# A new order table for the attention part, float64 conversion in three VectorE steps, and weight preparation moved

## The chip, the cores and the metric

The kernel runs on one core of a Trainium2 chip. Its engines work side by side, each through its own queue in program order: TensorE (PE) multiplies matrices, VectorE (DVE), ScalarE (ACT) and GpSimd (POOL) work element by element, SyncE (SP) issues most of the DMA transfers. The metric is the device time of one launch in microseconds (us); less is better.

## The reference

Attention with a learned position bias, for 4 batches, 8 heads, 576 positions and a head width of 64, then a block that mixes positions and applies an MLP. Cut to what is computed:

```python
scores = q @ k.T / sqrt(64) + bias        # bias[h,i,j] = relu(x[i,j]*w1 + b1) @ w2, hidden 32
attn = softmax(scores)                    # x = log1p(|i-j|) / log1p(max(i,1))
o = attn @ v                              # heads side by side: x is [4, 576, 512]
u = x + (x.T @ U @ V).T                   # mixes positions; U is 576x32, V is 32x576
out = u + relu(u @ w_ch1) @ w_ch2         # 512 -> 2048 -> 512
```

U, V, w_ch1 and w_ch2 come as float64. The kernel loads their two 32-bit words and puts a float32 together with bit operations.

## The kernel before, in words

**Stages.** First the bias table is built. Then come 16 pairs: a pair is one batch and two heads, p = 4 * batch + pair of heads. Then the MLP runs, its first steps (`m[0]`, `m[1]`, `y[0]`, ...) mixed with what is left of the last pair. The program is written with a manual schedule: each engine does its instructions in the order in which the code names them.

**A pair.** The 576 query rows of both heads make nine score tiles S0 to S8 (PE, L351); S0 holds the 64 middle rows of both heads. Each goes through T (DVE, L366: add the bias, find the maximum) and E (ACT, L384: exponential with row sums). The middle rows are normalised in PM (POOL, L405, two instructions, tile `pm`). X are transpositions on PE (L428, tile `tb`), C their copies out of PSUM (L411 on ACT, L413 on DVE); M and I are the same for the middle rows and the middle columns (tiles `tm`, `ti`), with CM and CI as their copies. AV0 and AV1 are the products with V (PE, L489), CO their copies (ACT), A0 and A1 transpose the outcome (tile `tx`), and D0 and D1 (DVE, L518, and for D0 also a small copy, L413) scale it into `x_sb`.

**Preparation of the next pair.** Q1 to Q4 split q and k of the next pair into a rounded part `hi` (L186) and a rest `lo` (L190) on POOL: hi of 1152 columns, lo of 1152, hi of 640, lo of 640. LA and LB are the loads of raw q and raw k for the pair after that, on SP's queue; the raw buffers are single, so such a load waits until the split of the pair before has read them.

**Float64 conversion.** From pair 2 on two jobs a pair are done, 20 in all (u, three pieces of v4, 16 pieces of the first MLP weights). VA: two steps on ACT (L206, L209). VD: clamp (DVE, L213) and shift (DVE, L218). VJ: join (DVE, L224) and the load of a later job. VP: add on POOL (L229) and what finishes the job before.

**Mix.** In pairs 5, 9 and 13, and after the last one, the four pairs of a batch are mixed: `mt` (PE, L538), `th` on ACT, `tl` on DVE, five products `mh` (PE, L560 to L562), five additions into `x_sb` (L566) and five stores to `u_dram`.

**What sets the order.** The table SLOTS names all of these for each slot 0 to 8 of a pair. One quote behind a name means the pair before, two quotes the one before that; `period(p, s)` walks through one slot. All outputs of PE take turns in one PSUM pool of four tiles, so that a new one waits until the one four places earlier has been emptied.

**Around it.** SP's list `loads` puts two more transfers into each slot (bias rows, raw q and k). In the last pairs `first_weights` brings in the converted first MLP weights, one step at a time (`next(feed, None)`): a load, a cast on ACT (L697, tiles `w1q`, `w2q`) and a subtraction on POOL (L698). `make_ut` (L687 to L690) transposes a block of u for the MLP.

Of the kernel before, what the change touches and what calls it, by code (L numbers as in the profile page):

```python
# [2 lines left out]

# [5 lines left out]
F32 = mybir.dt.float32  # L9
# [16 lines left out]
P = 128  # L26
# [15 lines left out]
CW = 256  # L42

SLOTS = (
    "S0 T8' D1'' E6' E7' E8'",
    "S1 T0 VD1' X20' E0 T1 MT MA C20' VP0' AV0' MD E1 N0 I1' CO0' H4 CI1' X30' VJ1' HD4 U4 H3 "
    "HD3 U3 N8' R8' C30' X31'",
    "S2 C31' Q1 H0 X21' C21' R0 PM",
    "S3 T2",
    "S4 HD0 U0 X00 T3 T4 VA0 H1 E2 E3 HD1 U1",  # L50
    "S5 AV1' E4 T5 C00 Q2 LA VD0 VJ0 A0' X11 Q3 CO1' I0 D0' C11 VP1' CI0 H2 HD2 U2 X01 X10 "
    "C01",
    "S6 M",
    "S7 C10 E5 Q4 LB",
    "S8 T6 T7 CM VA1 A1'",
)

CONV_FROM = 2
F64_LO = 2.0**-15
# [4 lines left out]
def kernel(  # L64
# [45 lines left out]

    ident = const.tile([P, P], F32, name="ident")
    sgn = const.tile([P, 1], I32, name="sgn")
    bits = const.tile([P, 8], I32, name="bits")
    three, mask, top = bits[:, 0:1], bits[:, 1:2], bits[:, 2:3].bitcast(F32)

    eps = const.tile([P, 9], F32, name="eps")[:, 0:1]
    u_sb = mix.tile([P, 5, RANK], F32, name="u_sb")
    v4h = mix.tile([P, 640], F32R, name="v4h")
    v4l = mix.tile([P, 640], F32R, name="v4l")
# [192 lines left out]
    def bias_loads(c, hp):  # L312

        h, r = 2 * hp, slice(c * P, min(S, (c + 1) * P))
        if c < 4:
            j = (1 + 2 * c) * S
            parts = [
                (bias[hp][:, j : j + S], bd[h][r]),
                (bias[hp][:, j + S + LEFT : j + 2 * S], bd[h + 1][r, 0 : S - LEFT]),
                (bias[hp][:, j + S : j + S + LEFT], bd[h + 1][r, S - LEFT : S]),  # L320
            ]
        else:
            parts = [(bias[hp][t * LEFT : (t + 1) * LEFT, 0:S], bd[h + t][r]) for t in range(2)]
        return [lambda o=o, i=i: nc.sync.dma_start(out=o, in_=i) for o, i in parts]
# [251 lines left out]
    def convert(what, k, p):  # L576

        j = 2 * (p - CONV_FROM) + k
        if p < CONV_FROM or j >= len(conv["jobs"]):
            return  # L580
        if j == 0 and what == "A":
            for i in range(3):
                conv["jobs"][i][0]()
        load, (size, low, clamp, shift, join, add), fin = conv["jobs"][j]
        if what == "A":
            size()
            low()
        elif what == "D":
            clamp()
            shift()  # L590
        elif what == "J":
            join()
            if j + 3 < len(conv["jobs"]):
                conv["jobs"][j + 3][0]()
        else:
            if j:
                conv["jobs"][j - 1][2]()
            add()
            if j == len(conv["jobs"]) - 1:
                fin()  # L600
# [3 lines left out]
    def do(name, p):  # L604

        k, a = name[0], [int(c) for c in name[1:] if c.isdigit()]
        if k in "MHU" and name not in ("M",):
            b = p // HP - 1
            if p > HP and p % HP == 1:
                {  # L610
                    "MT": mix_t, "MA": mix_hi, "MD": mix_lo,
                    "H": lambda: mix_add(*a) if name[1] == "D" else mix_h(*a),
                    "U": lambda: mix_store(b, *a),
                }[name if k == "M" else k]()
        elif k == "S":
            scores(p, *a)
        elif k == "T":
            add_bias(p, *a)
        elif k == "E":
            exps(p, *a)  # L620
        elif k == "N":
            add_eps(p, *a)
        elif k == "R":
            recip(p, *a)
        elif k == "P":
            norm_m(p)
        elif k == "X":
            tr(p, *a)
        elif name == "M":
            tr_m(p)  # L630
        elif name == "CM":
            tr_m_copy(p, "a")
        elif name[0:2] == "CI":
            tr_mid_copy(p, *a, "d")
        elif name[0:2] == "CO":
            av_copy(p, *a)
        elif k == "C":
            tr_copy(p, *a, "a" if a[0] == 3 or a[1] else "d")
        elif k == "I":
# [18 lines left out]
    def period(p, s):  # L658

        for x in SLOTS[s].split():  # L660
            q = p - x.count("'")
            if 0 <= q < NP and (x.strip("'"), q) not in done:
                do(x.strip("'"), q)

    def first(s):

# [169 lines left out]
        if i in early:  # L836
            first(early[i])
    loads[0:0] = bias_loads(3, 0)
    loads += bias_loads(1, 1) + bias_loads(2, 1) + [lambda: load_pair(2)] + bias_loads(3, 1)


    jobs = [(u32, 160, fin_u)]
# [15 lines left out]
    def first_weights(which):  # L858
        ys = []
        for k in range(KD + 2):  # L860
            if k < KD:
                ys.append(wrawp.tile([P, CW], I64, tag="wraw", name="y0").bitcast(F32))
                nc.sync.dma_start(out=ys[k], in_=wq_dram[4 * which + k])
            if k >= 2:
                split(0, which, k - 2, 0, DM)(ys[k - 2])
            yield

    feed = iter(())
    for p in range(NP):
        if p > 0:  # L870
            new_pair(p)
        if 0 < p < HP - 1:
            bias[p + 1] = big.tile([P, 9 * S], F32, tag=f"big{p + 1}", name=f"bias{p + 1}")
            loads = [o for c in (4, 0, 1, 2, 3) for o in bias_loads(c, p + 1)]
        for s in range(9):
            if s == 7 and 0 < p < NP - 1:
                load_v(p + 1)
            for o in loads[0:2]:
                o()
            del loads[0:2]  # L880
            period(p, s)
            if p == NP - 3 and s == 1:
                t = big.tile([P, 9 * S], F32R, tag="big0", name="w1q")
                *wq[0], uth[0] = big_views(t, [(WQ, KD), (WQ, KD), (LINE, None), (UT, KD)])
                feed = first_weights(0)
            if p == NP - 2 and s == 1:
                t = big.tile([P, 9 * S], F32R, tag="big1", name="w2q")
                w2a, w2b, utl[0] = big_views(t, [(WQ, KD), (WQ, KD), (LINE, None), (UT, KD)])
                wq[0] += [w2a, w2b]
                feed = first_weights(1)  # L890
            if p == NP - 1 and s == 1:
                t = big.tile([P, 9 * S], F32, tag="big2", name="acc")
                acc.update(enumerate(big_views(t, [(DM, 0)] * 10)))
                feed = iter(())
            if p >= NP - 3 and s in (1, 2, 4, 5, 7, 8):
                next(feed, None)
            if p == NP - 1 and s in (1, 2, 3, 4, 5):
                load_acc(2 * s - 2)
                load_acc(2 * s - 1)
            if p == NP - 1 and s in (6, 7):  # L900
                make_ut(0, s - 6)

    def run(*steps):
        for o in steps:
            o()
# [13 lines left out]
    utl[3], uth[4] = (x[:, LINE : LINE + UT].rearrange("p (k f) -> p k f", k=KD) for x in t)  # L919
    make_ut(1, 0)  # L920
    run(m[0][1])
    period(NP, 1)
    run(m[0][2])
    make_ut(1, 1)
    run(m[0][3])
# [7 lines left out]
    run(m[1][2])  # L933
    period(NP, 5)
    run(m[1][3])
    period(NP, 6)
    run(y[0][0])
    period(NP, 7)
    run(y[0][1])
    period(NP, 8)  # L940
    run(m[2][0])
    for s in range(9):
        period(NP + 1, s)
    mix_t()
    mix_hi()
    mix_lo()
    run(m[2][1])
    last_mix(4)
    run(m[2][2])
    last_mix(0)  # L950
    run(m[2][3])
    last_mix(1)
    run(y[1][0])
    last_mix(2)
    run(y[1][1])
    last_mix(3)
    p1.close()

    def pool(name, bufs):
# [103 lines left out]
```

## Time and profile before

| what | us |
|---|---|
| median of 3 runs | 770.46 |
| lowest, highest | 769.24, 772.63 |
| profiled execution | 765.32 |
| its span | 763.5 |
| PE busy in the span | 708.6 |
| DVE busy | 451.9 |
| ACT busy | 345.0 |
| POOL busy | 213.9 |

The span runs from the first to the last instruction that the profile shows; 1.8 us of the profiled execution lie outside. Busy time is an average over stages: up to about 58 us the bias table, up to about 335 us the 16 pairs, and from about 418 us on the MLP alone.

### The profile page before, as it was taken

How to read it: one execution, taken by the hardware profiler on the slowest of the kernel's cores; microseconds unless marked ns; L12 is line 12 of the kernel's file. 1: busy time of each engine (PE TensorE's matmuls, PEld its weight loads, DVE VectorE, ACT ScalarE, POOL GpSimd, SP SyncE). 2: the span in 40 equal slices, each digit the busy share in tenths (PEclk: the TensorE clock that was granted, in tenths of full speed). 3: DMA queues.
4: the chain of work that ended last, by engine and by line, in shares of the span. 5: the costliest groups of instructions: out<-in, count | busy, mean ns of one | idle time of the engine just before them, and what ended most of it. 6: DMA issues, size and time to landing. Idle time of an engine off the chain costs nothing.

```text
span 763.5 us, 15595 instructions
## 1 busy us (share of the span) xinstructions
PE 708.6 (93%) x6188; PEld 572.5 (75%) x6188; DVE 451.9 (59%) x964; ACT 345.0 (45%) x819; POOL 213.9 (28%) x222
## 2 busy tenths in 40 slices
PE   6886959989999997899989999999999999999998
PEld 3324747667667765587878998899899899889986
DVE  7994749899899876443389417852258721222222
ACT  6994659778868868641155203430133410011010
POOL 0011527556446636200055203640025500000000
PEclk9997979999999999999999999999999999999999
DMA  5898974456453445400522101320012100011111
GB/s 184 267 320 268 262 211 109 129 150 179 116 170 109 119 137 162 139 1 8 206 94 88 41 1 56 97 70 1 1 42 88 51 1 1 1 38 46 56 42 70
DMA packets 46520, 78.87 MB, mean 103 GB/s; under 512 B 7920, under 2 KB 14576, under 8 KB 46448
## 3 DMA queue, kind: packets, MB, share of 16 engines
q1 hardware_dynamic: 46208, 77.62, 32.6%
q8 instruction: 49, 0.80, 0.4%
q10 hardware_dynamic: 240, 0.26, 0.1%
q14 instruction: 23, 0.19, 0.1%
HBM read 55.43 MB, written 22.43 MB: 102 GB/s over the span
## 4 chain that ended last, share of the span: by engine, by line
PE 74%; DVE 11%; ACT 6%; DMA 4%; issue 3%; POOL 1%; SPq 1%; DVEq 0%; ACTq 0%; POOLq 0%
PE ph L714 25%; PE po L737 24%; PE o L489 8%; PE sc L351 6%; PE tb L428 3%; DVE p L366 3%; PE bs L287 3%; DVE wt L218 2%; DVE wt L224 1%; DVE wt L213 1%; ACT p L384 1%; PE mt L538 1%; ACT ring L275 1%; DVE pt L413 1%; PE mh L560 1%
## 5 line engine op out<-in xcount | busy, mean ns | idle before, releaser
L719 ACT ACTIVATE hh<-ph 128x1024 fp32r<-128x1024 f32 x36 | 36.9, 1025 | 205.2 <-PE ph L714 205.2
L720 DVE SCALAR_TENSOR_TENSOR hh<-ph,hh 128x1024 fp32r<-128x1024 f32 x36 | 44.1, 1225 | 139.7 <-ACT hh L719 139.7
L229 POOL TENSOR_TENSOR wy<-wt,wy 128x256 int32<-128x256 int32 (+1 forms) x68 | 53.3, 784 | 199.3 <-DVE wt L224 198.4
L737 PE MATMUL po<-w2q,hh 128*128 128x512 f32 x432 | 103.8, 395 | 0.0
L384 ACT ACTIVATE p<-p,st 128x576 f32<-128x576 f32 x128 | 98.5, 776 | 10.5 <-DVE st L366 10.2
L737 PE MATMUL po<-wq,hh 128*128 128x512 f32 x432 | 103.2, 395 | 0.0
L714 PE MATMUL ph<-ut,w1q 128*128 128x256 f32 x768 | 97.8, 285 | 2.3 <-DVE acc L740 1.9
L714 PEld LDWEIGHTS ph<-ut,w1q 128*128 128x128 f32 x768 | 95.2, 191 | 5.3 <-issue 3.4
L366 DVE CUSTOM_DVE_ANT_0 p<-sc,bias 128x576 f32<-128x576 f32 x128 | 91.4, 753 | 10.7 <-DMA bias<-bias_dram 5.5
L737 PEld LDWEIGHTS po<-w2q,hh 128*128 128x128 f32 x432 | 80.0, 188 | 18.0
L737 PEld LDWEIGHTS po<-wq,hh 128*128 128x128 f32 x432 | 80.2, 188 | 17.5
L714 PEld LDWEIGHTS ph<-ut,wq 128*128 128x128 f32 x768 | 90.9, 188 | 1.5
L740 DVE TENSOR_TENSOR acc<-po,acc 128x512 f32<-128x512 f32 x72 | 49.6, 689 | 70.7 <-PE po L737 70.7
L714 PE MATMUL ph<-ut,wq 128*128 128x256 f32 x768 | 91.2, 278 | 0.0
L489 PE MATMUL o<-pt,v 128*64 128x320 f32 (+1 forms) x640 | 88.0, 423 | 2.2 <-DVE st L366 1.6
L428 PE MATMUL tb<-ident,p 64*128 64x64 f32 x1024 | 53.0, 229 | 24.6 <-ACT p L384 10.8
L489 PEld LDWEIGHTS o<-pt,v 128*64 128x64 f32 x640 | 44.4, 141 | 35.9 <-issue 6.0
L428 PEld LDWEIGHTS tb<-ident,p 64*128 64x128 f32 x1024 | 44.5, 142 | 31.8 <-ACT p L384 11.2
L190 POOL TENSOR_TENSOR lo<-raw,hi 128x1152 fp32r<-128x1152 f32 (+1 forms) x30 | 64.3, 2144 | 0.3
L351 PE MATMUL sc<-hi 64*128 64x288 f32 (+1 forms) x320 | 59.2, 360 | 5.5 <-DVE w2q L690 1.4
L186 POOL TENSOR_SCALAR hi<-raw 128x1152 fp32r<-128x1152 f32 (+1 forms) x30 | 29.4, 981 | 95.8 <-DMA raw<-in_qk_dram 69.5
L287 PE MATMUL bs<-ring,small_sb 128*32 128x512 f32 (+17 forms) x352 | 43.0, 501 | 11.8 <-ACT ring L275 11.3
(95 smaller groups left out, 1051.6 us busy)
## 6 DMA issues: line engine op xcount, KB each, us to landing
wraw<-in_w_ch_dram SPq DMA_DIRECT2D x64, 256.0 KB, 2.8
raw<-in_qk_dram SPq DMA_DIRECT2D x32, 288.0 KB, 4.3
bias_dram<-ring SPq DMA_DIRECT2D x26, 295.5 KB, 3.5
v<-in_vp_dram SPq DMA_DIRECT2D x16, 320.0 KB, 4.6
bias<-bias_dram SPq DMA_DIRECT2D x16, 288.0 KB, 4.6
acc<-u_dram SPq DMA_DIRECT2D x18, 256.0 KB, 4.8
out_dram<-acc SPq DMA_DIRECT2D x18, 256.0 KB, 2.0
bias<-bias_dram SPq DMA_DIRECT2D x16, 256.0 KB, 4.9
```

Of the source, the lines that this page charges most:

```text
L190: eng.tensor_tensor(out=l, in0=raw, in1=h.bitcast(F32), op=ALU.subtract)
L229: nc.gpsimd.tensor_tensor(out=st["y"], in0=st["t"], in1=st["y"], op=ALU.add)
L287: mm(bs[T][32 * cg : 32 * cg + 32, a // 512, 0 : min(n - a, 512)], lhsT=w2_sb, rhs=hids[T][cg][:, a : min(n, a + 512)], start=True, stop=True,
L351: mm(ps[0:n, a, 0:HALF], lhsT=q[r, q0 : q0 + n], rhs=k[r, k0 : k0 + HALF], start=(i == 0), stop=(i == len(terms) - 1),)
L366: nc.vector.tensor_tensor_reduce(out=halves(dst), in0=d.pop(("ps", s))[:, :, 0:HALF], in1=halves(bias[p % HP][:, s * S : (s + 1) * S]), sc ...
L384: nc.scalar.activation(out=dst, in_=dst, func=AF.Exp, bias=st[:, s : s + 1], scale=-1.0, accum_out=st[:, 10 + s : 11 + s])
L428: nc.tensor.transpose(bank[:, h, i * D : (i + 1) * D], src[r, a : a + P], ident[r, r])
L489: mm(o[hd * D : (hd + 1) * D, 0:n], lhsT=v[:, vb * D : (vb + 1) * D], rhs=pt[:, pb, :], start=(j == 0), stop=(j == 4),)
L714: mm(st["ps"][:, f, :], lhsT=w, rhs=u[:, k, :], start=(i == 0), stop=(i == 3 * KD - 1))
L720: nc.vector.scalar_tensor_tensor(out=hl[n], in0=st["ps"], scalar=0.0, in1=hh[n].bitcast(F32), op0=ALU.max, op1=ALU.subtract)
L737: mm(ps, lhsT=h, rhs=w, start=(m == 0), stop=(m == 3 * FG - 1))
L740: nc.vector.tensor_tensor(out=a, in0=ps, in1=a, op=ALU.add)
```

## The change

The table SLOTS is new: every name but a few stands at another place, AV0, A0, A1 and D0, D1 stand up to two pairs behind the scores, and the last score tile has a slot of its own. A `^` behind a name means the pair ahead: Q1 stands in slot 8 for the split that is used two pairs later, and Q1 of pair 0 is done ahead of the loop. The copy C00 goes from DVE to ACT, so that DVE keeps C10 and C20. The shift of the conversion has a name of its own, VS. The first three float64 loads, which stood at VA of the first job in pair 2, stand in slots 0, 2 and 4 of pair 1. The q part and the k part of the raw loads of pair 2 have bias rows between them. `first_weights(0)` and `first_weights(1)` are one chain, of which 4 steps run in pair 13, 5 in pair 14 and 3 in pair 15, instead of six in each of pairs 13 and 14. The first two `make_ut` go from pair 15 to behind slots 0 and 1 of the period after it. In the tail the last addition and store of the mix stands ahead of `y[1][1]`. Constants of the conversion share a tile with `eps`.

```diff
 SLOTS = (
-    "S0 T8' D1'' E6' E7' E8'",
-    "S1 T0 VD1' X20' E0 T1 MT MA C20' VP0' AV0' MD E1 N0 I1' CO0' H4 CI1' X30' VJ1' HD4 U4 H3 "
...
+    "S0 R8'' A0'' T0 E5' CM' E7' VJ0' A1'' D0'' AV0' E8' E6' E0 I1' VS1' VP0' X21' CO0' D1'' "
+    "MT C21' VJ1' Q2 LA CI1' N0 MA",
...
+ON_DVE = ("C10", "C20")
...
-        if j == 0 and what == "A":
-            for i in range(3):
-                conv["jobs"][i][0]()
...
         elif what == "D":
             clamp()
+        elif what == "S":
             shift()
...
-            tr_copy(p, *a, "a" if a[0] == 3 or a[1] else "d")
+            tr_copy(p, *a, "d" if name in ON_DVE else "a")
...
-            q = p - x.count("'")
-            if 0 <= q < NP and (x.strip("'"), q) not in done:
-                do(x.strip("'"), q)
+            q, x = p - x.count("'") + x.count("^"), x.strip("'^")
+            if 0 <= q < NP and (x, q) not in done:
+                do(x, q)
...
-    loads += bias_loads(1, 1) + bias_loads(2, 1) + [lambda: load_pair(2)] + bias_loads(3, 1)
+    loads += bias_loads(1, 1) + bias_loads(2, 1) + [lambda: load_pair(2, 0)] + bias_loads(3, 1)
+    loads += [lambda: load_pair(2, 1)]
...
+            if p == CONV_FROM - 1 and s in (0, 2, 4):
+                conv["jobs"][s // 2][0]()
             period(p, s)
...
-                feed = first_weights(0)
+                feed = chain(first_weights(0), first_weights(1))
...
-                feed = first_weights(1)
...
-            if p >= NP - 3 and s in (1, 2, 4, 5, 7, 8):
+            if s in {NP - 3: (1, 2, 4, 7), NP - 2: (1, 3, 5, 7, 8), NP - 1: (1, 3, 5)}.get(p, ()):
                 next(feed, None)
...
-            if p == NP - 1 and s in (6, 7):
-                make_ut(0, s - 6)
...
     period(NP, 0)
+    make_ut(0, 0)
+    period(NP, 1)
+    make_ut(0, 1)
...
-    run(y[1][0])
-    last_mix(2)
+    for i, c in enumerate((4, 0, 1, 2, 3)):
+        run((m[2] + y[1])[i])
+        last_mix(c)
     run(y[1][1])
-    last_mix(3)
```

How the order moves on two engines, each as a row of the instruction (line, operation, tiles and shape). The first place is DVE in an ordinary pair, from the second job's clamp on (before):

```order
L213 SCALAR_TENSOR_TENSOR wt_2748<-wt_2748,bits_91 128x256
L218 SCALAR_TENSOR_TENSOR wt_2748<-wt_2748,bits_91 128x256
L224 SCALAR_TENSOR_TENSOR wt_2748<-wraw_2394,sgn_90,wt_2748 128x256
L518 TENSOR_TENSOR x_sb_96<-tx_2786,st_2317 128x2x128
L413 COPY x_sb_96<-tx_2786 64x128
L413 COPY pt_2775<-ti_2805 128x2x2x64
```

The same engine in the changed kernel, from the first job's join (`wt_2710`) to the second job's (`wt_2800`):

```order
L225 SCALAR_TENSOR_TENSOR wt_2710<-wraw_2375,sgn_90,wt_2710 128x256
L519 TENSOR_TENSOR x_sb_95<-tx_2891,st_2300 128x2x128
L414 COPY x_sb_95<-tx_2891 64x128
L219 SCALAR_TENSOR_TENSOR wt_2800<-wt_2800,eps_91 128x256
L519 TENSOR_TENSOR x_sb_95<-tx_2907,st_2300 128x2x128
L225 SCALAR_TENSOR_TENSOR wt_2800<-wraw_2617,sgn_90,wt_2800 128x256
L414 COPY pt_2948<-ti_2928 128x2x2x64
```

The three steps of a job stood in a row ahead of the scaling; now one job's join, the other's shift and its join stand on either side of the two scalings of the pair two back. The second place is POOL, one pair's worth, before:

```order
L186 TENSOR_SCALAR hi_2704<-raw_2490 128x1152
L405 TENSOR_SCALAR pm_2718<-praw_2631,st_2605 128x576
L405 TENSOR_SCALAR pm_2718<-praw_2631,st_2605 128x64
L190 TENSOR_TENSOR lo_2705<-raw_2490,hi_2704 128x1152
L186 TENSOR_SCALAR hi_2704<-raw_2579 128x640
L229 TENSOR_TENSOR wy_2597<-wt_2596,wy_2597 128x256
L190 TENSOR_TENSOR lo_2705<-raw_2579,hi_2704 128x640
L229 TENSOR_TENSOR wy_2749<-wt_2748,wy_2749 128x256
```

And in the changed kernel:

```order
L187 TENSOR_SCALAR hi_2573<-raw_2378 128x1152
L230 TENSOR_TENSOR wy_2423<-wt_2422,wy_2423 128x256
L191 TENSOR_TENSOR lo_2574<-raw_2378,hi_2573 128x1152
L230 TENSOR_TENSOR wy_2513<-wt_2512,wy_2513 128x256
L187 TENSOR_SCALAR hi_2573<-raw_2466 128x640
L191 TENSOR_TENSOR lo_2574<-raw_2466,hi_2573 128x640
L406 TENSOR_SCALAR pm_2790<-praw_2610,st_2588 128x576
L406 TENSOR_SCALAR pm_2790<-praw_2610,st_2588 128x64
```

The normalisation `pm` stood between hi and lo of q; now it stands behind both halves of the split, and the 1152-column lo stands between the adds of the two jobs. The third place is POOL in pairs 14 and 15, where the first weights are split; before:

```order
L186 TENSOR_SCALAR hi_4773<-raw_4560 128x1152
L405 TENSOR_SCALAR pm_4787<-praw_4704,st_4678 128x576
L405 TENSOR_SCALAR pm_4787<-praw_4704,st_4678 128x64
L698 TENSOR_TENSOR w2q_4762<-y0_4763,w2q_4762 128x512
L190 TENSOR_TENSOR lo_4774<-raw_4560,hi_4773 128x1152
L186 TENSOR_SCALAR hi_4773<-raw_4652 128x640
L698 TENSOR_TENSOR w2q_4762<-y0_4790,w2q_4762 128x512
L190 TENSOR_TENSOR lo_4774<-raw_4652,hi_4773 128x640
```

And in the changed kernel:

```order
L191 TENSOR_TENSOR lo_4646<-raw_4415,hi_4645 128x1152
L697 TENSOR_TENSOR w1q_4441<-y0_4509,w1q_4441 128x512
L187 TENSOR_SCALAR hi_4645<-raw_4527 128x640
L697 TENSOR_TENSOR w1q_4441<-y0_4634,w1q_4441 128x512
L191 TENSOR_TENSOR lo_4646<-raw_4527,hi_4645 128x640
L406 TENSOR_SCALAR pm_4844<-praw_4681,st_4659 128x576
L406 TENSOR_SCALAR pm_4844<-praw_4681,st_4659 128x64
L697 TENSOR_TENSOR w2q_4747<-y0_4813,w2q_4747 128x512
L697 TENSOR_TENSOR w2q_4747<-y0_4903,w2q_4747 128x512
L697 TENSOR_TENSOR w2q_4747<-y0_4923,w2q_4747 128x512
L697 TENSOR_TENSOR w2q_4747<-y0_5015,w2q_4747 128x512
L406 TENSOR_SCALAR pm_5121<-praw_4949,st_4927 128x576
```

The two splits of `w1q` have moved into pair 14, ahead of its `pm`, and the `pm` of pair 15 stands behind all four splits of `w2q`.

## Rows read from the trace of the kernel before

**Rows 1.** Stretches: us, busy PE, PEld, DVE, ACT, POOL, PEclk, DMA, GB/s.

```profile
86.43:111.11 24.68, 14.96 (x196) 12.11 (x192) 11.94 (x34) 12.74 (x34) 8.67 (x8) 0.79 0.84 242
...
111.11:270.09 158.98, 148.49 (x1983) 107.02 (x1980) 144.85 (x374) 127.84 (x335) 89.08 (x83) 1.00 0.47 135
...
125.24:161.13 35.89, 33.64 (x414) 23.00 (x410) 31.91 (x79) 26.67 (x70) 20.48 (x21) 1.00 0.47 137
...
175.61:190.08 14.47, 13.21 (x196) 10.09 (x193) 13.66 (x37) 12.48 (x34) 9.11 (x9) 1.00 0.49 144
...
418.00:763.50 345.50, 341.79 (x2186) 308.20 (x2184) 142.27 (x200) 68.28 (x136) 57.94 (x71) 1.00 0.12 39
```

**Rows 2.** PE's waits: who for whom, us in total, times, longest; then its timeline.

```profile
PE tb L428 <- DVE x_sb L413: 9.9, 9, 1.3
...
268.12 2.04 PE L538 MATMUL mt<-x_sb,u_sb 128*32 128x512 f32 x10
```

**Rows 3.** The hole in pair 2 and what follows, as stretches, and ACT's wait.

```profile
104.75:109.60 4.85, 4.85 (x62) 4.82 (x64) 3.00 (x9) 3.83 (x10) 0.09 (x1) 0.50 0.81 231
95.03:104.75 9.72, 0.00 (x0) 0.00 (x0) 1.62 (x5) 2.90 (x9) 3.63 (x4) 0.72 1.02 314
...
ACT wt L206 <- DMA wraw<-in_u_dram: 10.4, 1, 10.4
```

**Rows 4.** Stretches: the windows of pairs 12 to 14, then the tail.

```profile
270.09:330.80 60.71, 52.19 (x611) 38.40 (x610) 35.39 (x94) 39.73 (x97) 23.97 (x21) 0.94 0.38 125
...
374.00:418.00 44.00, 39.64 (x246) 35.14 (x245) 32.58 (x55) 19.89 (x50) 20.84 (x26) 0.96 0.42 138
```

**Rows 5.** Timelines of POOL and SP's queue (SPq): start, us, instruction, [idle before <- releaser].

```profile
91.15 1.16 POOL L186 TENSOR_SCALAR hi<-raw 128x1152 fp32r<-128x1152 f32 x1 [7.84 <-DMA raw<-in_qk_dram]
92.29 1.05 POOL L405 TENSOR_SCALAR pm<-praw,st 128x576 f32<-128x576 f32 x2
...
95.89 0.72 POOL L186 TENSOR_SCALAR hi<-raw 128x640 fp32r<-128x640 f32 x1
...
82.01 2.23 SPq L147 DMA_DIRECT2D raw<-in_qk_dram  x2
...
86.99 3.68 SPq L153 DMA_DIRECT2D raw<-in_qk_dram  x4
...
96.57 0.43 SPq L199 DMA_DIRECT2D wraw<-in_u_dram  x1
```

**Rows 6.** DVE, two ordinary pairs: line, count, busy us, mean ns, idle before.

```profile
L413 DVE COPY pt<-tb 128x512 f32<-128x512 f32 x6 | 4.1, 687 | 0.1
L218 DVE SCALAR_TENSOR_TENSOR wt<-wt,bits 128x256 int32<-128x256 int32 x4 | 2.6, 654 | 0.1
L224 DVE SCALAR_TENSOR_TENSOR wt<-wraw,sgn,wt 128x256 int32<-128x256 int32 x4 | 2.6, 654 | 0.1
...
L213 DVE SCALAR_TENSOR_TENSOR wt<-wt,bits 128x256 f32<-128x256 f32 x4 | 2.2, 540 | 0.0
```

**Rows 7.** Timeline of DVE and POOL near 218 (one job's three steps).

```profile
217.92 0.41 DVE L213 SCALAR_TENSOR_TENSOR wt<-wt,bits 128x256 f32<-128x256 f32 x1
217.98 1.77 POOL L190 TENSOR_TENSOR lo<-raw,hi 128x640 fp32r<-128x640 f32 x1
218.37 1.66 DVE L218 SCALAR_TENSOR_TENSOR wt<-wt,bits 128x256 int32<-128x256 int32 x1
...
220.07 0.48 DVE L224 SCALAR_TENSOR_TENSOR wt<-wraw,sgn,wt 128x256 int32<-128x256 int32 x1
```

**Rows 8.** POOL in the two ordinary pairs, by line and shape.

```profile
L190 POOL TENSOR_TENSOR lo<-raw,hi 128x1152 fp32r<-128x1152 f32 x2 | 5.3, 2668 | 0.0
```

**Rows 9.** POOL, 290 to 331 us, by line and shape: splits of first weights.

```profile
L698 POOL TENSOR_TENSOR w2q<-y,w2q 128x512 fp32r<-128x512 f32 x4 | 5.1, 1282 | 2.1 <-ACT w2q L697 2.1
```

**Rows 10.** Tail, 366 to 420 us: ACT's wait, and a step of the chain.

```profile
ACT wt L206 <- DMA wraw<-in_w_ch_dram: 7.7, 1, 7.7
...
367.51 2.79 PE po L737 x12
```

More of the change, by code (lines that the diff above doesn't have):

```diff
@@ L1 @@
 from contextlib import ExitStack
-from itertools import count
+from itertools import chain, count
 import concourse.bass as bass
@@ L44 @@
 SLOTS = (
-    "S0 T8' D1'' E6' E7' E8'",
-    "S1 T0 VD1' X20' E0 T1 MT MA C20' VP0' AV0' MD E1 N0 I1' CO0' H4 CI1' X30' VJ1' HD4 U4 H3 "
[L47 to L55, printed above, removed]
[10 rows of a table added]
 )
+ON_DVE = ("C10", "C20")
 CONV_FROM = 2
@@ L112 @@
     sgn = const.tile([P, 1], I32, name="sgn")
-    bits = const.tile([P, 8], I32, name="bits")
-    three, mask, top = bits[:, 0:1], bits[:, 1:2], bits[:, 2:3].bitcast(F32)
-    eps = const.tile([P, 9], F32, name="eps")[:, 0:1]
+    consts = const.tile([P, 9], F32, name="eps")
+    eps, top = consts[:, 0:1], consts[:, 1:2]
+    three, mask = consts[:, 2:3].bitcast(I32), consts[:, 3:4].bitcast(I32)
     u_sb = mix.tile([P, 5, RANK], F32, name="u_sb")
@@ L868 @@
     feed = iter(())
+    for x in " ".join(SLOTS).split():
+        if x.endswith("^"):
+            do(x.strip("^"), 0)
     for p in range(NP):
@@ L893 @@
                 acc.update(enumerate(big_views(t, [(DM, 0)] * 10)))
-                feed = iter(())
-            if p >= NP - 3 and s in (1, 2, 4, 5, 7, 8):
+            if s in {NP - 3: (1, 2, 4, 7), NP - 2: (1, 3, 5, 7, 8), NP - 1: (1, 3, 5)}.get(p, ()):
                 next(feed, None)
@@ L921 @@
     run(m[0][1])
-    period(NP, 1)
     run(m[0][2])
@@ L935 @@
     run(m[1][3])
[L936 to L943, printed above, removed]
+    for n in range(NP, NP + 2):
+        for i in range(6 if n == NP else 0, 9):
+            period(n, i)
+        run(y[0][n - NP])
     mix_t()
@@ L946 @@
     mix_lo()
[L947 to L952, printed above, removed]
-    run(y[1][0])
-    last_mix(2)
+    for i, c in enumerate((4, 0, 1, 2, 3)):
+        run((m[2] + y[1])[i])
+        last_mix(c)
     run(y[1][1])
-    last_mix(3)
     p1.close()
```

8 rows, old and new, of the table SLOTS are left out of this document.

## The prediction

> **What bounds the kernel now.** I read the windows first. From 418 to the end (the MLP) TensorE (PE) works 341.79 of 345.50 us at full clock, so nothing can be won there [rows 1]. What the change touches lies before: ten windows from the first AV0 (the attention-times-V product) of one pair to that of the next. A window without a mix takes 14.47 us, in which PE is busy 13.21, VectorE (DVE) 13.66, ScalarE (ACT) 12.48 and GpSimd (POOL) 9.11 [rows 1]. No engine is full, so next I asked who ends the waits. PE waits nine times, 9.9 us in all and at most 1.3, for the small copy into x_sb that empties a transposed output tile [rows 2]. PSUM has four tiles in rotation, so PE's next tile needs the one four allocations back emptied, and that copy stands behind three conversion steps on DVE. So DVE sets the pace of an ordinary pair, and PE's 13.2 us are the floor under it. Outside these windows there are two larger holes: PE idle for 9.72 us from 95.03, while ACT stands at a conversion ahead of the exponential that PE needs [rows 3], and three windows near the end, 60.71 us with 52.19 of PE's work [rows 4].
>
> **Part one: the first float64 loads.** ACT stands 10.4 us at the first conversion because that load lands late [rows 3]. SyncE (SP) issued it at 96.57, after bias and raw loads [rows 5]. The hole is PE's 9.72 us; behind it PE worked 4.85 us at a granted 0.50 [rows 3], the 1.2 GHz level of its two (1.2 and 2.4 GHz), work for 2.4 us at full clock, so 2.4 more were lost. Removed: 12.1 us. With the loads in pair 1 they are issued some 15 to 20 us sooner, and their landing is no longer what comes last. What is next late: the middle rows. The new order puts POOL's normalisation (pm) of pair 2 behind both halves of pair 3's split. Of that, the raw k half is issued on SP at 86.99 for 3.68 us [rows 5]. In a stretch where the 16 DMA engines are 84% busy [rows 1], raw q went from its issue at 82.01 to a first use at 91.15 [rows 5], about 9 us; k so lands at about 95.5 to 96. Then hi (0.72) and pm (1.05) [rows 5] and between them the 640-column lo (1.77 [rows 7]) give 99.0 to 99.5. PE would want pm about 10.5 us behind AV0 of pair 1 (86.43 [rows 1], plus all of the pair's 13.2 us but the last scores and transpositions): at 97. A new stall of some 2 to 3 us, taken as 2.5, and, as behind the old one, 2.4 us of slow clock. **Net gain 12.1 − 2.5 − 2.4 = 7.2**, bounds 4 (the k half lands 3 us later) and 12 (no stall at all). The three loads cost SP three issues of about 0.43 us [rows 5], beside other work.
>
> **Part two: the ten windows.** They took 158.98 us [rows 1]. At their end the mix of pair 13 already had 2.0 us of PE's work in it (`mt` [rows 2]), which the new order does later, so I compare with 157.0.
> ACT gets copy C00: DVE loses 0.69 [rows 6]; ACT comes to about 13.1, still under the pace. Clamp, shift and join cost 0.540, 0.654 and 0.654 in the mean [rows 6], 1.85 per job and 3.70 per pair with two jobs. The means hide a pattern: where POOL ran nothing, the three took 0.41, 0.48 and 0.48; the shift that began at 218.37, while POOL's lo ran from 217.98 for 1.77, took 1.66 and ended 0.28 after lo did [rows 7]. So I count the bare steps, 2 × 1.38 = 2.76, and add each meeting with POOL by itself. Bare DVE work: 13.66 − 0.69 − (3.70 − 2.76) = 12.03.
> Now the meetings. In the new order POOL does the add of the first job and straight behind it the 1152-column lo, 2.67 us [rows 8], while DVE does the second job's shift and join. The shift meets the add (+0.2). The join stands one 0.42 us scaling behind it, so comes about 0.5 us into lo and waits for the rest: 2.67 − 0.5 + 0.28 − a little, 2.1. Before, the long lo stood beside work that it doesn't hold up. Clamp and first shift meet little (+0.2). With 0.3 us idle: 12.03 + 2.5 + 0.3 = 14.85 per ordinary pair. AV0 and the assembly run a pair later, which takes the x_sb copy's stall off PE, but PE then waits for whatever DVE frees last.
> The Trainium skill has the rule for this: "SBUF — State Buffer", section "Who interferes with whom", says that DVE and GpSimd share one port pair as an exclusive lock, and that who issues first keeps it for the whole instruction. By the mean rows a pair would be near 13.6, by the lock 14.85; the one long shift sides with the lock.
> A mix adds 7.22 us of PE work spread over two windows (33.64 against 2 × 13.21) [rows 1]; now it falls into one, 13.21 + 7.22, at least 20.43, taken as 20.5, and the DVE work fits under it. Pair 12 has fewer conversion steps left: 14.4. Sum: 7 × 14.85 + 14.4 + 2 × 20.5 = 159.4 against 157.0: **loss 2.4**. Bounds: with the mean prices a gain of 7; if two more steps meet POOL, a loss of 16 (both below).
>
> **Part three: pairs 13 to 15.** The windows of pairs 12 to 14 [rows 4] lose 60.71 − 52.19 = 8.5 us of idle PE, and by their granted clock of 0.94 another 0.06 × 60.71 = 3.6. Spreading the first MLP weights (each split 1.28 on POOL [rows 9], with a cast on ACT ahead of it) over three pairs takes the splits out of the scores' way. But pm of pair 14 now stands behind a lo, two splits and another lo, and pm of pair 15 behind the third w2q split, whose cast stands behind the pair's fourth exponential. My walk along the new order leaves waits of 1.85 and 3.15 us there, 1.7 of slow clock, 2.3 at make_ut and the last mix, and about 1 that a slower pair loses to DVE: 10 of 12.1 come back. **Gain 2**, bounds −2 and +6.
>
> **Part four: the tail.** The last store of u now goes ahead of y[1][1], 12 matmuls of together 2.79 us [rows 10]. Behind it come the loads for which ACT waits 7.7 us [rows 10]; PE has 4.4 us idle between 374 and 418 [rows 4], and a load 2.8 sooner fills only part of it. The reordered first steps of the MLP leave PE's count as it is. **Gain 1.5**, bounds 0 and 4.
>
> **Sum.** 7.2 − 2.4 + 2 + 1.5 = 8.3 us. The profiled execution took 765.32 (a span of 763.5 and 1.8 outside), 5.1 under the median; against its time it is 757.0, against the median 770.46 − 8.3 = 762.2.
>
> **Rivals.**
> *Meetings with POOL cost little.* If join slips in ahead of lo, or lo is slowed instead, the pair goes to PE's floor with small losses, 13.6, and pair 12 to 13.5: 7 × 13.6 + 13.5 + 41 = 149.7, a gain of 7.3. Total 18.0: 752.5. For it: the means are low, and only some steps of a pair are long. Against: here the order itself sets join half a microsecond behind lo's start. Chance 0.2.
> *Gains given back to transfers and to pm.* Raw k of pair 3 lands 3 us later, since the three float64 loads are now ahead of it on SP, and pm in pairs 14 and 15 costs what the old splits did: 4 − 2.4 + 0 + 0.5 = 2.1, so 768.3, no change that can be told. For it: DMA is 84% busy there. Chance 0.2.
> *More steps meet POOL: slower.* Clamp and shift of the first job stand near Q4 and Q1, a 640-column lo (1.77 [rows 7]) and an 1152-column hi (1.16 [rows 5]). If each meets its own in the middle, they wait 0.88 + 0.28 and 0.58 + 0.28, and with the 0.2 taken off a pair is 16.7: 7 × 16.7 + 14.4 + 41 = 172.3, a loss of 15.3. Total 7.2 − 15.3 + 2 + 1.5 = −4.6: 775.1. It decides from 16.6 us per ordinary pair on. Against: POOL is busy only 9.11 of 14.47 [rows 1]. Chance 0.1.
>
> **How the numbers follow.** Main case 0.5, its own range 757 to 768 by the bounds of the terms; the three rivals 0.2, 0.2, 0.1. A difference under 0.5% (766.6 to 774.3) can't be told from no change. Faster: 0.2 of the first rival and 0.48 of the main case, 0.68. Same: 0.02 of the main case and most of the second rival with a little of the third, 0.21. Slower: 0.11 with the bad ends of all. The range leaves out the lower half of the first rival and the last: 751 to 772.
>
> **What would show it.** Right: no wait of ACT for the u32 load; ordinary pairs of 14.6 to 15.1 us; the second job's join near 2.5 us, ending 0.28 us behind the long lo; PE waits of 2 to 3 us for pm in pair 2 and in pairs 14 and 15. Wrong: join at 0.5 us and pairs near 13.5 (first rival); pairs above 16.5 with long clamps and shifts (third); a hole near 97 us that is 5 us or more (second); or a stall of PE for an output tile that the deeper order keeps in PSUM, which I have priced at nothing.

## The result

The changed kernel takes 750.4 us (median of 4 runs, 748.99 to 752.36) against 769.85 of the kernel before in the same comparison (4 runs, 766.7 to 772.63): a ratio of 0.975, 95% interval 0.9705 to 0.9795. It is faster by 19.5 us where 8.3 was forecast, and 0.6 us below the lower end of the range. The profiled execution took 750.97 us with a span of 749.2, against 763.5 before: 14.3 us less. The kernel before ran 44 times beside all kernels of this study, with a median of 767.6 (764.7 to 772.6): its profiled execution (765.32) is one of its shorter ones, and the median that the prediction started from one of the longer. The traces so have 14.3 us to explain. Of the 5.2 that are left of the 19.5, 4.5 are the distance of the kernel before's profiled execution from the median that it is compared by here, and 0.6 that of the changed kernel's: scatter from one execution to the next, not the change.

### The profile after

Stretches of the changed kernel (us, busy time and count of PE, PEld, DVE, ACT, POOL, granted clock, DMA share, GB/s): an ordinary pair from AV0 to AV0; the ten windows from AV0 of pair 2 to that of pair 12; one of these, from AV0 of pair 3; the windows of pairs 12 to 14; 4.61 us behind a stall in pair 1; a steady block of the MLP.

```profile
170.68:185.44 14.76, 13.23 (x197) 10.09 (x193) 14.22 (x36) 13.12 (x35) 8.87 (x8) 1.00 0.52 139
...
102.82:264.62 161.80, 149.08 (x1974) 108.83 (x1970) 146.30 (x362) 132.49 (x342) 90.08 (x85) 0.98 0.51 144
117.19:133.94 16.75, 14.71 (x197) 11.40 (x193) 14.00 (x38) 14.59 (x40) 9.95 (x10) 0.91 0.39 109
...
264.62:316.09 51.47, 46.99 (x594) 33.75 (x590) 33.50 (x93) 40.08 (x99) 24.18 (x21) 0.97 0.48 147
...
83.79:88.40 4.61, 4.61 (x56) 4.54 (x58) 3.11 (x9) 2.98 (x8) 1.15 (x1) 0.50 1.04 326
...
613.72:624.86 11.14, 11.14 (x74) 10.17 (x73) 2.62 (x4) 1.03 (x1) 0.00 (x0) 1.00 0.01 1
```

The hole of 9.72 us and the wait of ACT [rows 3] are gone. The ordinary pair has grown from 14.47 to 14.76 [rows 1], though DVE lost a copy; the ten windows take 161.80 instead of 158.98. The three windows of pairs 12 to 14 take 51.47 instead of 60.71 [rows 4]. PE's longest waits behind the bias table changed their names. The first column is who waits for whom, then us in all, times, and the longest:

```profile
PE sc L352 <- DVE pt L414: 10.3, 7, 1.6
PE ti L429 <- POOL pm L406: 8.8, 4, 2.9
PE ph L713 <- DVE acc L739: 3.1, 3, 1.4
```

The wait for the x_sb copy (9.9 us in nine stalls, [rows 2]) has become one of 10.3 in seven for another small DVE copy, `pt<-ti`, which also empties a PSUM tile. What holds up that copy stands right ahead of it on DVE. DVE, then POOL, around 188 us (start, us, instruction):

```profile
187.21 0.70 DVE L219 SCALAR_TENSOR_TENSOR wt<-wt,eps 128x256 int32<-128x256 int32 x1
187.83 0.41 DVE L519 TENSOR_TENSOR x_sb<-tx,st 128x256 f32<-128x256 f32 x1
188.16 2.52 DVE L225 SCALAR_TENSOR_TENSOR wt<-wraw,sgn,wt 128x256 int32<-128x256 int32 x1
190.61 0.41 DVE L414 COPY pt<-ti 128x256 f32<-128x256 f32 x1
...
186.89 0.73 POOL L230 TENSOR_TENSOR wy<-wt,wy 128x256 int32<-128x256 int32 x1 [1.55 <-issue]
187.58 2.82 POOL L191 TENSOR_TENSOR lo<-raw,hi 128x1152 fp32r<-128x1152 f32 x1
```

The second job's join began 0.58 us behind POOL's long lo, took 2.52 instead of 0.48 [rows 7], and ended at 190.68, 0.28 behind the end of lo. That is the meeting that the prediction counted, at the place and of the size it gave, and it is what the Trainium skill's "SBUF — State Buffer", "Who interferes with whom", says of the shared ports. It is there in eight of the ten windows, at 2.52 or 2.53 us each time. Mean prices would have hidden it again: in two ordinary pairs the mean of the four joins is 1.500 us, over two of 0.47 to 0.48 and two of 2.52 to 2.53.

### Where the time went, stage by stage

To compare kernels whose orders differ I counted PE's matmuls, each with the mean time of its kind at full clock, and read at equal work how far the changed kernel is ahead of the kernel before:

| stage (us in the kernel before) | forecast | measured in the traces |
|---|---|---|
| first loads and the hole, to 127 | +7.2 | +7.2 |
| ten windows, 127 to 268 | −2.4 | −4.9 |
| pairs 13 to 15, 268 to 334 | +2 | +5.5 |
| tail, 334 to 435 | +1.5 | +3.0 |
| steady MLP, from 435 | 0 | +3.4 |
| sum | 8.3 | 14.3 |

The rows are rounded one by one. The first term holds and the second has the right sign; two fall short by 3.5 and 1.5, and the last was not in the sum at all. Each row is read from one execution of each kernel.

### The profile page after: what moved, and what is told of

Its sections match the earlier page's. It is cut to its first block, busy times and chain, and to the rows that moved or that the text cites. A ratio compares the mean times of both kernels' runs of the same rounds, so it can differ in the third digit from the quotient of the medians.

```text
span 749.2 us, 15583 instructions
## 1 busy us (share of the span) xinstructions
PE 702.7 (94%) x6188; PEld 570.6 (76%) x6188; DVE 450.3 (60%) x948; ACT 354.3 (47%) x835; POOL 215.1 (29%) x222
## 4 chain that ended last, share of the span: by engine, by line
PE 72%; DVE 9%; ACT 5%; issue 4%; POOL 4%; DMA 4%; SPq 1%; DVEq 0%; POOLq 0%; ACTq 0%
PE ph L713 25%; PE po L736 24%; PE sc L352 6%; PE o L490 6%; PE tb L429 3%; PE bs L288 3%; DVE wt L225 3%; POOL lo L191 1%; DVE wt L219 1%; PE mt L539 1%; PE mh L561 1%; DMA wraw<-in_w_ch_dram 1%; DMA raw<-in_qk_dram 1%; ACT ring L276 1%; POOL wy L230 1%
## 5 line engine op out<-in xcount | busy, mean ns | idle before, releaser
L736 PE MATMUL po<-w2q,hh 128*128 128x512 f32 x432 | 102.0, 391 | 0.0
L367 DVE CUSTOM_DVE_ANT_0 p<-sc,bias 128x576 f32<-128x576 f32 x128 | 93.3, 752 | 13.4 <-DMA bias<-bias_dram 7.7
L713 PE MATMUL ph<-ut,w1q 128*128 128x256 f32 x768 | 94.7, 280 | 3.4 <-DVE acc L739 3.1
L713 PEld LDWEIGHTS ph<-ut,w1q 128*128 128x128 f32 x768 | 92.6, 188 | 6.3 <-issue 4.5
L352 PE MATMUL sc<-hi 64*128 64x288 f32 (+1 forms) x320 | 60.0, 368 | 11.9 <-DVE pt L414 10.3
L412 ACT COPY pt<-tb 128x512 f32<-128x512 f32 x96 | 55.2, 587 | 27.6 <-PE tb L429 25.9
```

Of the source, the lines that this page charges most:

```text
L352: mm(ps[0:n, a, 0:HALF], lhsT=q[r, q0 : q0 + n], rhs=k[r, k0 : k0 + HALF], start=(i == 0), stop=(i == len(terms) - 1),)
L367: nc.vector.tensor_tensor_reduce(out=halves(dst), in0=d.pop(("ps", s))[:, :, 0:HALF], in1=halves(bias[p % HP][:, s * S : (s + 1) * S]), sc ...
L412: nc.scalar.copy(out=out, in_=in_)
L713: mm(st["ps"][:, f, :], lhsT=w, rhs=u[:, k, :], start=(i == 0), stop=(i == 3 * KD - 1))
L736: mm(ps, lhsT=h, rhs=w, start=(m == 0), stop=(m == 3 * FG - 1))
```

## The experiments

### The MLP's pace: 32 bytes

The steady MLP has the same instructions in both kernels, yet one block took 11.35 us before and 11.14 after. The one edit that reaches it is the merged tile of constants: everything behind it on the left side of SBUF lies 32 bytes lower. Two runs exchange that alone, a third moves it the other way:

```diff
 # b_layout: the kernel before with
-    bits = const.tile([P, 8], I32, name="bits")
...
-    eps = const.tile([P, 9], F32, name="eps")[:, 0:1]
+    consts = const.tile([P, 9], F32, name="eps")
...
 # a_layout: the changed kernel with the two old lines
 # b_pad: the kernel before with
-    bits = const.tile([P, 8], I32, name="bits")
+    bits = const.tile([P, 16], I32, name="bits")
```

> The kernel before with one edit of the change alone: the conversion's constants share the tile of eps, so that every tile behind it on the left side of SBUF lies 32 bytes lower, as in the changed kernel. No instruction moves. The traces show that the steady MLP blocks (one hh tile to the next) took 11.35 us each in the kernel before and 11.13 in the changed one at places where the same tiles are used, 3.4 us over the MLP in all, which no step of the prediction priced. Theory (addresses set PE's pace): blocks of 11.13, 3 to 4 us less. Rival (chance from one execution to the next): blocks differ without a pattern, and the median stays within 1 us of the kernel before.

> The changed kernel with the two tiles of constants apart again, so that its MLP tiles lie where those of the kernel before lay. Theory (addresses set PE's pace): blocks of 11.35 us instead of 11.13, 3 to 4 us more, near 754. Rival (chance): no change, near 750.5.

> The kernel before with its tile of constants 32 bytes longer, so that every tile behind it on the left side lies 32 bytes higher (64 above the changed kernel's) and no instruction moves. Theory (what counts is that the left tiles' addresses are, like those of the right side, 32 above a multiple of 64): steady blocks of 11.13 us, as 32 bytes lower. Rival (a lower address, or its remainder to 128 or more, counts): blocks of 11.35 or of yet another length.

One steady block, first of the kernel before, then of b_layout, a_layout and b_pad (columns as above):

```profile
626.83:638.18 11.35, 11.35 (x74) 10.27 (x73) 2.61 (x4) 1.03 (x1) 0.00 (x0) 1.00 0.01 1
```

```profile
627.57:638.70 11.13, 11.13 (x74) 10.16 (x73) 2.61 (x3) 1.03 (x1) 0.00 (x0) 1.00 0.01 1
```

```profile
614.43:625.78 11.35, 11.35 (x74) 10.27 (x73) 2.61 (x3) 1.03 (x1) 0.00 (x0) 1.00 0.01 1
```

```profile
629.49:640.76 11.27, 11.27 (x74) 10.20 (x73) 2.60 (x3) 1.03 (x1) 0.00 (x0) 1.00 0.01 1
```

PE is busy without a gap at full clock and with the same number of matmuls in all four, POOL stands still and DMA hardly moves; only the pace differs, and it follows the layout. From 435 us of the kernel before to the last block, b_layout gains 3.06 us on it, and so does the changed kernel. Of the 28 blocks there 16 are quicker, by 0.09 to 0.27 us each, and 12 take the same to 0.01. In medians b_layout took 765.36 against 768.11 (ratio 0.997, interval 0.9951 to 0.9989), and a_layout 754.11, 3.7 above the changed kernel. The theory that addresses set the pace is shown. Its finer form, that the remainder to 64 counts, falls with b_pad (one execution): 32 bytes higher is 11.27, not 11.13. Which property of an address counts is open.

### The early loads alone

```diff
 # b_early: the kernel before with
-        if j == 0 and what == "A":
-            for i in range(3):
-                conv["jobs"][i][0]()
...
+            if p == CONV_FROM - 1 and s in (0, 2, 4):
+                conv["jobs"][s // 2][0]()
```

> The kernel before with the first three float64 loads issued in pair 1 at slots 0, 2 and 4, all else as it was. Theory (the late load alone makes the hole of 9.72 us and the slow clock behind it): the hole goes, 9 to 12 us less, since in the old order the middle rows' normalisation does not stand behind pair 3's split; near 759. Rival (something else is late right behind it, a bias or raw load that the three loads push back): 3 to 7 us less, and a new hole between 90 and 110 us.

It took 763.5 us against 768.11 (ratio 0.9938, interval 0.991 to 0.9965), 4.6 less: the size of the rival. The profiled execution, 765.4, is one of its longer ones, so the trace tells where the time goes and not how much is left. At equal work it is 7.1 us ahead behind the old hole and 4.3 of that are gone one pair later. PE's waits between 90 and 120 us:

```profile
PE tb L428 <- DVE x_sb L413: 3.0, 1, 3.0
PE ti L428 <- POOL pm L405: 2.2, 1, 2.2
```

The wait for pm, at 95.7, is a new hole in the stretch that the rival named; with a granted clock of 0.65 over the 4.94 us behind it, it is most of why 7.1 are gained there and not 12.1. The longer wait comes later, at 113.6. What stands ahead of it, on POOL and DVE:

```profile
110.48 1.15 POOL L186 TENSOR_SCALAR hi<-raw 128x1152 fp32r<-128x1152 f32 x1 [7.26 <-DMA raw<-in_qk_dram]
...
111.81 0.83 DVE L213 SCALAR_TENSOR_TENSOR wt<-wt,bits 128x256 f32<-128x256 f32 x1
...
112.78 2.85 POOL L190 TENSOR_TENSOR lo<-raw,hi 128x1152 fp32r<-128x1152 f32 x1
...
113.19 2.72 DVE L224 SCALAR_TENSOR_TENSOR wt<-wraw,sgn,wt 128x256 int32<-128x256 int32 x1
...
116.59 0.69 PE L428 MATMUL tb<-ident,p 64*128 64x64 f32 x8 [3.01 <-DVE x_sb L413]
```

POOL stands 7.26 us until raw q of the next pair lands, so its split is late against DVE: the long lo begins 0.97 behind the job's clamp, where in the kernel before, at the same place, it began 2.16 ahead of it (116.47 and 118.63). The join then meets lo and takes 2.72 us, and the x_sb copy behind it comes late. DVE itself is not late: from the first job's join to this clamp it took 3.96 us, and 3.95 in the kernel before. Whether the three loads pushed raw q back, as the rival has it, or the pair now merely comes sooner than the load can, this run does not separate. The loads alone are worth less than the hole; at the same place the changed kernel still has 7.2 of its lead.

### The join and the long lo

Two edits of the changed kernel test DVE as the pace of a pair: one takes the join out of lo's way by doing the second job's add (which needs the join) first on POOL, the other gives DVE the copy C00 back.

```diff
 # a_vp1: the changed kernel with
-    "MT C21' VJ1' Q2 LA CI1' N0 MA",
+    "MT C21' VJ1' VP1' Q2 LA CI1' N0 MA",
...
-    "S2 H4 T1 VP1' X30' ...
+    "S2 H4 T1 X30' ...
 # a_c00: the changed kernel with
-ON_DVE = ("C10", "C20")
+ON_DVE = ("C00", "C10", "C20")
```

> The changed kernel with the second job's add on POOL (VP1') moved ahead of the 1152-column lo (Q2), so that the second job's join no longer meets that lo. Theory (the join waits for POOL's running lo, 2 us a pair, and DVE so sets the pace): join 0.5 us instead of 2.5, ordinary pairs 13.4 to 13.7 instead of 14.75, 8 to 10 us less than the changed kernel, near 741. Rival (PE waits for the output tiles whatever the join takes, or the lo that now comes 1.5 us later makes pm or the scores late): ordinary pairs above 14.3, within 3 us of the changed kernel.

> The changed kernel with the copy C00 back on DVE. Theory (DVE with its wait for POOL sets the pace of the changed kernel's ordinary pairs): 0.69 us more in most pairs, 15.3 to 15.5 instead of 14.76, 5 to 8 us more in all, near 757. Rival (PE or ACT sets it, DVE has room): within 1.5 us of 750.4.

a_vp1 took 744.95 us (ratio to the kernel before 0.970, interval 0.9664 to 0.9735), 5.5 under the changed kernel by medians and 7.3 by spans (741.9 against 749.2). An ordinary pair of it, and its join around 183 us with POOL's work:

```profile
166.75:180.67 13.92, 13.33 (x197) 10.21 (x193) 12.82 (x36) 12.94 (x35) 8.80 (x8) 1.00 0.56 148
```

```profile
183.39 0.47 DVE L225 SCALAR_TENSOR_TENSOR wt<-wraw,sgn,wt 128x256 int32<-128x256 int32 x1
184.00 0.73 POOL L230 TENSOR_TENSOR wy<-wt,wy 128x256 int32<-128x256 int32 x1 [1.14 <-ACT praw L385]
184.69 2.67 POOL L191 TENSOR_TENSOR lo<-raw,hi 128x1152 fp32r<-128x1152 f32 x1
```

The join is down to 0.47, and the pair is 0.84 us shorter, not the 1.1 to 1.4 expected: a wait of 0.56 for pm takes part of it. The whole lies between what theory (8 to 10) and rival (at most 3) gave; the theory's mechanism holds, its size doesn't. a_c00 took 758.92 (ratio 0.9878, interval 0.9845 to 0.9912), 8.5 more than the changed kernel, and its ordinary pair 15.49 with DVE busy 14.70:

```profile
180.26:195.75 15.49, 13.73 (x195) 10.29 (x193) 14.70 (x37) 12.84 (x35) 8.86 (x9) 1.00 0.48 134
```

0.73 us more in a pair for a copy of 0.69 on DVE: DVE with its wait for POOL sets the pace, as expected, and the whole is a little over the 5 to 8 us that the theory gave.

### pm ahead of the second half of the split

```diff
 # a_vp1_pm: a_vp1 with
-    "S2 ... VA0 R0 H1 X20'",
+    "S2 ... VA0 R0 PM H1 X20'",
-    "S6 T5 AV1' X01 PM I0 ...
+    "S6 T5 AV1' X01 I0 ...
```

> The changed kernel with two edits: the second job's add (VP1') ahead of the 1152-column lo, as in the run before this one, and the middle rows' normalisation (pm) moved from slot 6 to slot 2, right behind its reciprocal, so that POOL does it ahead of the 640-column lo and, in pairs 14 and 15, ahead of most weight splits. Theory (what is left of the pairs' waits is pm: 0.56 us in each ordinary pair, 2.3, 1.9, 1.5 and 2.5 in pairs 2, 4, 14 and 15, with slow clock behind some): ordinary pairs 13.3 to 13.4 us instead of 13.92, 6 to 11 us less than that run's 744.95, near 736. Rival (the lo that comes later, or POOL standing at a reciprocal that is late, makes the next scores wait): within 3 us of 744.95, with PE waits for lo.

734.39 us (ratio 0.9573, interval 0.9538 to 0.9608), 10.6 under a_vp1 by medians (7.0 by spans, 734.9 against 741.9) and 16 under the changed kernel: the fastest kernel of this study. PE's waits for pm in a_vp1, where the changed kernel had 8.8 us in four:

```profile
PE ti L429 <- POOL pm L406: 12.0, 11, 2.5
```

And in a_vp1_pm, with the new wait for a DVE copy:

```profile
PE ti L429 <- POOL pm L406: 2.6, 4, 1.6
...
PE tb L429 <- DVE pt L414: 2.2, 5, 0.5
```

An ordinary pair from AV0 to AV0 is 13.56 to 13.6, somewhat more than the 13.3 to 13.4 expected, with that new wait of 0.4 to 0.5. The place of pm, which the prediction named as the thing that is next late, was worth more, once the join was out of lo's way, than any one part of the change. It was not tried without VP1'.

### Pairs 13 to 15: which edit made the gain

Five runs undo one thing each, or two:

```diff
 # a_feed: first weights as in the kernel before
...
-            if s in {NP - 3: (1, 2, 4, 7), NP - 2: (1, 3, 5, 7, 8), NP - 1: (1, 3, 5)}.get(p, ()):
+            if p >= NP - 3 and s in (1, 2, 4, 5, 7, 8):
 # a_ut: first two make_ut in pair 15
+            if p == NP - 1 and s in (6, 7):
+                make_ut(0, s - 6)
...
 # a_q34: Q3 from S2 to S5, Q4 LB from S5 to S7
 # a_qall: also Q1 from S8 of the pair ahead to the end of S1, Q2 LA from S0 to S5
 # a_qall_feed: a_qall and a_feed
```

> The changed kernel with the first MLP weights fed as in the kernel before (six steps in pair 13, six in pair 14, from slots 1, 2, 4, 5, 7 and 8). Theory (spreading the weights made the gain of 5.5 us that the trace shows in pairs 13 to 15): scores wait again for POOL's lo behind the splits, 3 to 6 us more than the changed kernel, 754 to 756. Rival (the gain came from Q1 a pair ahead and from make_ut's new place): within 1.5 us of 750.4.

> The changed kernel with the first two make_ut back in pair 15, slots 6 and 7. Theory (they stalled PE there, 1.4 and 1.2 us, and their new place hides that): 1.5 to 3 us more than the changed kernel, near 752.5. Rival (another wait takes their place, the pm of pair 15): within 1 us.

> The changed kernel with the k half of the split back where the kernel before had it: Q3 in slot 5 and Q4 with its load in slot 7, instead of slots 2 and 5. Theory (the earlier split, not the spread weights, took the scores' waits for POOL out of pairs 13 to 15, which gained 5.5 us of PE's progress): PE waits again for lo and hi at the first scores of pairs 14 and 15, 3 us or more lost there, and 2 us or more over the whole run, though pm now comes earlier. Rival (the gain there has another cause): no wait of PE for lo or hi between 280 and 330 us, and a time at or below 750.4 since pm stands earlier.

> The changed kernel with all four steps of the split back at the places of the kernel before: Q1 at the end of slot 1, Q2 with its load and Q3 in slot 5, Q4 with its load in slot 7. Weights are fed as in the changed kernel. Theory (that the split starts a slot or more ahead of the pair is what took the scores' waits for POOL out of pairs 13 to 15): PE waits again for lo or hi at the first scores of pairs 14 and 15, at least 2 us together, and of the 5.5 to 8 us that these pairs gain no more than 4 are left. Rival (the gain there comes from the rest of the table): no such wait, and the gain stays. In ordinary pairs the long lo now meets the bias steps and no join: shorter pairs, 13.5 to 14.

> The run before this one with the weights also fed as in the kernel before, so that POOL's work in pairs 13 to 15 stands nearly as it did. Theory (the early split or the spread weights, either alone, suffices): the waits for lo and hi come back here in full, 3 us or more at pairs 14 and 15, also if a_qall shows none. Rival (the rest of the table made the gain): no such waits in either run.

| kernel | median us | ratio to the kernel before, interval | gain in pairs 13 to 15, at equal work |
|---|---|---|---|
| changed | 750.4 | 0.975, 0.9705 to 0.9795 | 5.5 |
| a_feed | 750.53 | 0.9785, 0.9763 to 0.9807 | 6.6 |
| a_ut | 750.31 | 0.9787, 0.9743 to 0.983 | 5.3 |
| a_q34 | 747.06 | 0.9732, 0.9703 to 0.9761 | 8.1 |
| a_qall | 745.91 | 0.9723, 0.9692 to 0.9753 | 2.7 |
| a_qall_feed | 747.02 | 0.9724, 0.9679 to 0.9769 | 2.0 |

The theories for a_feed, a_ut and a_q34 fell: spreading the weights, make_ut's place and the place of the k half gain nothing there. Two other runs of this study that leave these pairs as they are in the changed kernel, a_layout and a_tail, lie within 0.3 of it by this count. The gain goes below 4 only when the split's first half, Q1 and Q2, stands late again, so at least half of it (2.8 of 5.5; 5.4 counted from a_q34) hangs on their early start; what makes the rest, no run separates. The wait did not come back under its old name, though. PE's waits between 262 and 335 us, of the changed kernel, then of a_qall:

```profile
PE ti L429 <- POOL pm L406: 4.0, 2, 2.5
PE ph L713 <- ACT w1q L688: 0.7, 1, 0.7
PE ph L713 <- DVE w2q L689: 0.3, 1, 0.3
```

```profile
PE ti L429 <- POOL pm L406: 5.9, 3, 2.5
```

In the new table pm is wanted before lo is, so a POOL that is late shows as a wait for pm. Here a_qall's expectation of a wait for lo was wrong, that of the size right, and a_qall_feed's wait for lo and hi did not come either. a_q34 and a_qall are also faster than the changed kernel as a whole. In a_qall the long lo no longer starts beside the second join, and its ordinary pair takes 13.9 (AV0 to AV0); in a_q34, whose pairs take 15.0, pm stands ahead of the last lo and the stall of 1.86 at 127 us and that of 1.46 in pair 14 are gone.

### The tail

```diff
 # a_tail: the changed kernel with
-    for i, c in enumerate((4, 0, 1, 2, 3)):
-        run((m[2] + y[1])[i])
-        last_mix(c)
...
+    (the lines of the kernel before: y[0][1] and m[2][0] ahead of the last period,
+     last_mix(3) behind y[1][1])
```

> The changed kernel with the steps behind slot 5 of the last period in the order of the kernel before (last mix addition and store behind y[1][1], m[2][0] ahead of the last period). Theory (the store ahead of y[1][1] brings the loads behind it sooner): the wait of ACT for them grows by about 2.8 us and 1.5 to 3 us are lost between 365 and 410 us, near 752.5. Rival (that order changes nothing that PE waits for): within 1 us of 750.4.

753.8 us (ratio 0.9816, interval 0.9785 to 0.9848), 3.4 more than the changed kernel by medians and 2.9 by spans. ACT's wait for the load behind the store, in the changed kernel and in a_tail:

```profile
ACT wt L207 <- DMA wraw<-in_w_ch_dram: 5.8, 1, 5.8
```

```profile
ACT wt L207 <- DMA wraw<-in_w_ch_dram: 8.3, 1, 8.3
```

In a_tail PE then stands for `hh`, which ACT and DVE make behind these conversions, and the matmuls that follow run at a granted 0.77 (380.05 to 387.40), 7.42 us where the changed kernel takes 5.89:

```profile
378.96 0.66 PE L686 MATMUL tu<-ident,acc 128*128 128x128 f32 x4 [2.25 <-DVE hh L719]
380.05 7.42 PE L713 MATMUL ph<-ut,w1q 128*128 128x256 f32 x48 [0.43 <-DVE acc L739]
```

With the new order of the tail the load comes 2.5 sooner, and about as much reaches PE: at equal work a_tail's tail gains nothing on the kernel before. The run puts back the first MLP steps together with the store, so it does not show which of the two brings the load sooner.

## Why the prediction was wrong

The forecast of 8.3 and the measured 19.5 are 11.2 apart: 3.5 in pairs 13 to 15, 1.5 in the tail and 3.4 in the steady MLP were missing, the ten windows lost 2.5 more than forecast, and 5.2 are the two executions' distance from their medians.

**The first loads: right in size, with the stall a pair off, which is in part luck.** Net 7.2 as forecast. The new stall for pm came, 2.94 us, with 4.61 us at a granted 0.50 (the 1.2 GHz level) behind it. It came in pair 1, not in pair 2:

```profile
83.79 0.37 PE L429 MATMUL ti<-ident,pm 64*128 64x64 f32 x2 [2.94 <-POOL pm L406]
```

POOL ended pm at 83.74, behind both halves of pair 2's split. In pair 2, where the prediction worked the stall out, POOL ended pm at 97.69 and PE asked for it at 99.36: PE came late itself and lost nothing. A stall that was not priced has the size of the one that was.

**The ten windows: the mechanism right, 2.5 us too little loss.** The ordinary pair was forecast at 14.85 and takes 14.76, the mix windows at 20.5 and they take 20.4 and 20.1. What was missing are two windows of 16.75 and 16.36: in the first PE waits 1.86 us for pm and the clock is granted 0.91 of full in the mean; the second has a wait of 1.6 for the DVE copy, with a like stretch of slow clock behind it. The second belongs to this execution: a_ut and a_tail, which have the same order up to there, take 14.8 in its place, and all three have the first. Without it the loss would be about 3. The step "7 × 14.85" took all pairs as alike; the stall that the prediction put a price on in pairs 2, 14 and 15 stands in pair 4 as well.

**Pairs 13 to 15: the step that failed was what is left over.** Of 12.1 us the prediction left 10; 6.7 were left. The waits for pm, forecast at 1.85 and 3.15, are 1.46 and 2.51, and the slow clock is the 1.7 expected; but 2.3 for make_ut and the last mix are 1.0, and the 1 for a slower DVE is nothing. The cause given for the gain, the spread weights, was wrong: a_feed takes it away without loss. At least half of the gain hangs on the earlier start of Q1 and Q2, an effect of the table that the prediction left unpriced there; late again, they cost through pm (5.9 us of waits instead of 4.0) and not through lo. The rest stays open.

**The tail: half of what it gave.** "A load 2.8 sooner fills only part" was the wrong choice between the bounds of 0 and 4: the wait for it is 5.8 in the changed kernel and 8.3 with the old order put back into it (7.7 in the kernel before), and the tail gains 3.0.

**The steady MLP: not in the sum.** "Nothing can be won there" was read from a busy share of 99%. PE was full, but not as fast as it can be: the same matmuls run 1 to 2% quicker in 16 of 28 blocks once the tiles lie elsewhere. The merged constants stood in the diff, and the prediction gave them no term.

**The scale.** The sum was made on the profiled execution and put against a median 5.1 us above it, as if each gained alike. Over 44 runs the distance is 2.3. This is the larger part of why the runs shown first moved by 19.5 and the traces by 14.3.

The first rival came out near the measured time (752.5) and for the wrong reason: its 13.6 us a pair did not occur in the changed kernel, and the meeting of join and lo that it denied is there in eight of the ten windows. The range ended at 751.0 because it took its lower end from half of that rival, and the terms that were short, 3.5, 1.5 and 3.4, all lay on one side.

## What to carry to other kernels

Where two engines block each other, look for the order in which their long instructions start, not at mean durations: one small step moved past a 2.7 us instruction was worth 5.5 us here by medians (7.3 by spans), and putting a short producer (pm) ahead of a long one on the same queue was worth 10.6 more (7.0 by spans). When an engine is busy 99% of a stage, compare how long one of its instructions takes in different blocks of that stage before calling the stage fixed; and give every edit that changes an allocation a term, even if no instruction moves. A wait that disappears under one name should be looked for under the next output that the same late engine makes.

## What the runs showed of the hardware

The pace of fp32r matmuls depends on where their tiles lie in SBUF, at a granted clock of 1.00 and with POOL and DMA at rest: a block of 74 records took 11.13, 11.35 and 11.27 us with the left side's tiles 32 bytes lower, as in the kernel before, and 32 bytes higher, and the same 11.35 or 11.13 to 0.01 us in every kernel of the first two layouts. Twelve other blocks take the same, to 0.01 us, in those two. What about an address matters was not found.

A join on DVE that takes 0.47 us alone takes 2.52 or 2.53 when it begins 0.58 us into POOL's 1152-column lo, and ends 0.28 behind it: eight times in the changed kernel.
